# The experts' second layer in 320 and 192 columns instead of 256 and 256, with its weight units cut along k

## The chip, the cores and the metric

One core of one Trainium2 chip runs the whole program. The metric is the device time of one execution in microseconds (us); the times named here are of the kernel before. A profiled execution gives the trace, whose own clock starts at 0 and ends with the span.

## The reference, cut to what matters

Three layers follow each other: linear attention, a gated feed-forward layer, and a soft mixture of eight experts. Only the last one is touched:

```python
N, D, E, S_per_e, F = (2304, 512, 8, 4, 1024)
...
for e in range(E):
    h = np.maximum(slot_input[e] @ w1[e], 0.0)
    slot_out[e] = h @ w2[e]
slot_out = slot_out.reshape(n_slots, D)
c = logits - logits.max(1, keepdims=True)
c = np.exp(c)
c /= c.sum(1, keepdims=True) + 1e-09
return (c @ slot_out).astype(np.float32)
```

w1 and w2 are 16 MB each. An expert has four slots, so that its two products have four rows each; the combination `c @ slot_out` makes 2304 rows of 512 columns from 32 slots.

## The kernel before, in words

The front of the program (attention, the gated layer in six blocks of 384 tokens) is the same in both versions; the change lies in the tail, from about 680 us on, in the block that begins with `with ExitStack() as p3`.

**Weights.** w1 and w2 come in 32 units of 1 MB, a tile `eu` of 128 x 2048 each. `unit(n)` gives unit n and, where it isn't there yet, asks for all units up to n: each takes a place in one of the pools xw, wpA, wpB, xl (24 places in turn) and a load on SyncE's queue (L710). A load waits until the place's last reader is done. Units 0 to 15 are w1 (half of F, expert), 16 to 31 are w2. In w2, unit 16+e holds, for expert e, all eight k slices of 128 rows and the first 256 columns; unit 24+e holds the other 256 columns. Units 0 to 23 are asked for before the tail begins.

**First layer.** `fc1(e, half)` (L1081) multiplies the slots' inputs `xo` by one unit: four products of 512 columns, each in its own 32 output partitions. `turn1(half)` (L1086) copies the sums, turns them on TensorE (tile hp), adds over k and fills the tile `ho` with the ReLU. In the middle of the first half, before expert 4 (CTURN), `cturn` turns the last block's combine weights (ctp, cb), writes them to DRAM (`cT_d`, L826, on SyncE's queue) and `load_c` asks ScalarE's queue for both halves of the whole table cT, 432 KB each.

**Second layer.** `fc2(e, r, half)` (L1096) makes four of the eight k slices for expert e and column half r: four products of 256 columns into y2[r]. TensorE takes all of r = 0 first (eight experts with k slices 0 to 3, then eight with 4 to 7), then r = 1, expert by expert. A product of F32 operands stands in the trace as two records.

**Slots and combination.** `slots(r)` (L1103) copies y2[r] to SBUF, sums over partitions by a product with istack (tile so), and scales it into SO on VectorE in two operations. `combine(r, i)` (L1114) makes 256 tokens: two products of cT with SO (F32R, one record each), a copy from PSUM by VectorE or ScalarE in turn, and a transfer of 256 KB to `out` on SyncE's queue, in pieces of 1 KB. From expert 4 on (ELEFT), two combinations of r = 0 (NLEFT) follow each expert's products of r = 1; the last of them and all nine of r = 1 follow after `slots(1)`.

The order on an engine comes from a scheduler that goes by priorities; `placed(f, engine)` ties what f traces to the engine's last instruction, so that the written order stands there.

Of the kernel before, what the change touches and what calls it, by code (L numbers as in the profile page):

```python
# [7 lines left out]
F32 = mybir.dt.float32  # L8
# [3 lines left out]
ALU = mybir.AluOpType  # L12
# [15 lines left out]
LOW = 0.93 * 2.0 ** -29  # L28
KCONV, MCONV = (3, 2), (2, 2)
NX = 4  # L30
NLEFT = 2
ELEFT = 4
CTURN = 4
CEVERY = 3
PSLOTS = [1, 4, 7, 12, 14, 16, 18, 20, 24]
# [30 lines left out]
def tile_kernel(ctx: ExitStack, tc: tile.TileContext, q2T, qT, kT, v, wbd, wg, wv, wo, rmsg, phi, w1, w2, consts, out):  # L66
# [637 lines left out]
    def unit(n):  # L704
        while len(units) <= n:
            k = len(units)
            r, e = divmod(k, NE)
            u = upool[k % len(upool)].tile([128, 2048], F32, tag="w", name=f"eu{k}")
            src = (w1 if r < 2 else w2)[e, r % 2]
            SP.dma_start(out=u, in_=src)  # L710
            units.append(u)
        return units[n]
# [25 lines left out]
    with ExitStack() as p2:  # L738
# [10 lines left out]
        def post(blk, x2):  # L749
# [67 lines left out]
                DVE.tensor_copy(c3[:, :, 1], c3[:, :, 0])  # L817
                DVE.tensor_tensor(out=c3[:, :, 2].bitcast(F32R), in0=c, in1=c3[:, :, 0], op=ALU.subtract)

            def cturn(tp=None, keep=None):  # L820
                tp = tp or post_tile("ctp", [96, TPB, 128])
                for o in range(TPB):
                    PE.transpose(out=tp[:, o], in_=st["c3"][:, o].rearrange("p r s -> p (r s)"), identity=ident)
                cb = (keep or sp).tile([96, BLK], F32, tag="row", name="cb", bufs=1)
                DVE.tensor_copy(cb, tp.rearrange("p o t -> p (o t)"))
                SP.dma_start(out=cT_d[:, blk * BLK:(blk + 1) * BLK], in_=cb)  # L826

            def finish(acc, late):

# [235 lines left out]
    with ExitStack() as p3:  # L1065
        sp = pool(p3, "sp3")
        ps = pool(p3, "ps3", PSUM)
        y2 = [ps.tile([128, 256], F32, name=f"y2{r}") for r in range(2)]
        y1 = [ps.tile([128, 512], F32, tag="op", name=f"y1{r}", bufs=5) for r in range(2)]
        SO = sp.tile([96, 2, 256], F32R, name="SO")  # L1070
        cT = []

        ho = Own(8, wpA.tile([128, 8 * NE * NS], F32, tag="w", name="ho"))
# [1 line left out]
        def load_c():  # L1075
            for n in range(2):
                t = wpA.tile([128, NT // 2], F32R, tag="w", name="cT")[0:96]
                ACT.dma_start(out=t.bitcast(F32), in_=cT_d[:, NT // 2 * n:NT // 2 * n + NT // 2])
                cT.append(t)
# [14 lines left out]
            ho.fill(lambda o, i: ACT.activation(out=o, in_=i, func=AF.Relu), h, 4 * half, 4 * half + 4)  # L1094

        def fc2(e, r, half):  # L1096
            u = unit((2 + r) * NE + e).rearrange("p (k d) -> p k d", k=8)
            for c in range(4):
                k = 4 * half + c
                PE.matmul(out=y2[r][32 * c:32 * c + 32], lhsT=ho[e, k], rhs=u[:, k],  # L1100
                          start=e == 0 and half == 0, stop=e == NE - 1 and half == 1)

        def slots(r):  # L1103

            ysum = sp.tile([128, 256], F32, tag="y2s", name="y2s", bufs=1)
            DVE.tensor_copy(ysum, y2[r])
            so = ps.tile([96, 256], F32, tag="so", name="so", bufs=1)
            PE.matmul(out=so, lhsT=istack, rhs=ysum, start=True, stop=True)
            DVE.tensor_scalar(out=SO[:, r], in0=so, scalar1=rz, scalar2=None, op0=ALU.mult)
            DVE.scalar_tensor_tensor(out=SO[32:64, r], in0=so[32:64], scalar=rz[32:64], in1=SO[32:64, r].bitcast(F32), op0=ALU.mult, op1=ALU.subtract)  # L1110

        obs = {}

        def combine(r, i):  # L1114
            if i % 3 == 0:
                obs[r] = wpB.tile([128, 3, 2, 256], F32, tag="w", name="ob")
            ob = obs[r][:, i % 3]
            op = ps.tile([128, 2, 256], F32, tag="op", name="op", bufs=5)
            for n in range(2):
                t = 2 * i + n  # L1120
                PE.matmul(out=op[:, n], lhsT=cT[t // 9][:, 128 * (t % 9):128 * (t % 9) + 128], rhs=SO[:, r], start=True, stop=True)
            if i % 2:
                DVE.tensor_copy(ob, op)
            else:
                ACT.copy(out=ob, in_=op)
            SP.dma_start(out=out[256 * i:256 * i + 256, 256 * r:256 * r + 256].rearrange("(n p) d -> p n d", n=2), in_=ob)

        for e in range(NE):
            if e == CTURN:
                lastturn(ps.tile([96, TPB, 128], F32, tag="op", name="ctp", bufs=5), kl)  # L1130
                load_c()
            fc1(e, 0)
        fc1(0, 1)
        turn1(0)
        for e in range(1, NE):
            fc1(e, 1)
        for e in range(2):
            fc2(e, 0, 0)
        turn1(1)
        for e in range(2, NE):  # L1140
            fc2(e, 0, 0)
        for e in range(NE):
            fc2(e, 0, 1)
        first = [lambda i=i: combine(0, i) for i in range(TILES // 2)]
        for e in range(NE):
            fc2(e, 1, 0)
            fc2(e, 1, 1)
            if e == 0:
                slots(0)
            for f in first[:NLEFT] if e >= ELEFT else ():  # L1150
                f()
            first = first[NLEFT:] if e >= ELEFT else first
        slots(1)
        for f in first:
            f()
# [4 lines left out]
def _layout(inputs):  # L1160
    import numpy as np

    def heads(a):
# [22 lines left out]
        "rmsg": np.asarray(inputs["moe_rms_g"]).reshape(4, 128).T,  # L1186
        "phi": np.asarray(inputs["moe2_phi"]).reshape(4, 128, NS).transpose(1, 0, 2).reshape(128, 4 * NS),
        "w1": np.asarray(inputs["moe2_w1"]).reshape(NE, 4, 128, 2, 512).transpose(0, 3, 2, 1, 4).reshape(NE, 2, 128, 2048),
        "w2": np.asarray(inputs["moe2_w2"]).reshape(NE, 8, 128, 2, 256).transpose(0, 3, 2, 1, 4).reshape(NE, 2, 128, 2048),
        "consts": consts,  # L1190
    }

# [19 lines left out]
```

## Time and profile before

| what | value |
|---|---|
| time, median of 3 runs | 731.23 us (728.85 to 732.27) |
| the profiled execution's own time | 730.81 us |
| its span | 729.0 us, 11925 instructions |
| mean granted clock of TensorE | 0.991 |
| TensorE busy (PE) | 706.5 us, 97% |
| VectorE, ScalarE, GpSimd busy | 447.2, 340.5, 170.2 us |
| DMA of the whole span | 79.43 MB, mean 109 GB/s |
| chain that ended last, by engine | PE 84%, DVE 7%, ACT 4%, issue 2%, POOL 1%, DMA 1% |

The shares are averages over the whole program; TensorE is the bound of the six blocks, which the change leaves as they are. What counts here is the tail, where the weights of the experts come in and the result goes out; there the windows and the timelines of the single engines are read.

### The profile page before, as it was taken

Reading aid. Unit: us, or ns where it says so; the run is one execution under the profiler, and the core shown is the slowest. Engines: PE = TensorE matmul, PEld = TensorE weight load, DVE = VectorE, ACT = ScalarE, POOL = GpSimd, SP = SyncE. Lnnn points to the kernel's source line nnn. Section 1 sums busy time; section 2 is a strip of 40 time slices with the busy share of each in tenths; the row PEclk is TensorE's granted clock in tenths of the full one; section 3 lists DMA queues with packets and bytes.
Section 4 is the critical chain, followed back from the end, with each engine's and each line's share of the span. In section 5 each row is a group of like instructions: output and inputs, shape, how many; then the busy total and the mean of one; then the engine's idle time right before and its main releaser. Section 6 shows DMA issues by size and latency. Waiting matters only on the chain.

```text
span 729.0 us, 11925 instructions
## 1 busy us (share of the span) xinstructions
PE 706.5 (97%) x4713; PEld 575.7 (79%) x4713; DVE 447.2 (61%) x874; ACT 340.5 (47%) x711; POOL 170.2 (23%) x84
## 2 busy tenths in 40 slices
PE   6999999999999999999999999999999999999994
PEld 4657766988889888898889888899887999898343
DVE  5899755798655565566776666766667653233313
ACT  5896755698444554355531545415454131212103
POOL 0233200234101210124443244342443300000000
PEclk9999999999999999999999999999999999999898
DMA  8684214443011000100000100001000066576798
GB/s 315 215 293 171 88 37 160 150 181 119 1 62 39 27 22 23 39 22 22 23 1 9 44 22 23 1 9 33 23 1 1 9 259 260 201 261 265 280 371 273
DMA packets 25143, 79.43 MB, mean 109 GB/s; under 512 B 2688, under 2 KB 13376, under 8 KB 18688
## 3 DMA queue, kind: packets, MB, share of 16 engines
q1 hardware_dynamic: 24864, 77.79, 30.0%
q10 hardware_dynamic: 224, 0.88, 0.4%
q8 instruction: 37, 0.61, 0.3%
q14 instruction: 18, 0.15, 0.1%
HBM read 71.99 MB, written 6.67 MB: 108 GB/s over the span
## 4 chain that ended last, share of the span: by engine, by line
PE 84%; DVE 7%; ACT 4%; issue 2%; POOL 1%; DMA 1%; SPq 0%; DVEq 0%; POOLq 0%; ACTq 0%
PE pv L938 20%; PE pg L938 19%; PE acc L963 6%; PE acc L964 6%; PE acc L965 6%; PE num L221 4%; PE kacc L571 4%; PE y L1084 2%; PE P L526 2%; PE kacc L580 2%; PE y L1100 2%; DVE wt L154 2%; DVE wt L156 1%; PE o L472 1%; ACT wt L144 1%
## 5 line engine op out<-in xcount | busy, mean ns | idle before, releaser
L938 PE MATMUL pv<-xnh,wv 128*128 128x384 f32 x576 | 152.3, 345 | 0.0
L938 PE MATMUL pg<-xnh,wg 128*128 128x384 f32 x576 | 150.1, 342 | 0.5 <-DVE t L946 0.3
L938 PEld LDWEIGHTS pv<-xnh,wv 128*128 128x128 f32 x576 | 102.7, 188 | 12.3 <-issue 7.8
L938 PEld LDWEIGHTS pg<-xnh,wg 128*128 128x128 f32 x576 | 104.7, 188 | 6.2 <-ACT xnh L119 0.6
L938 PE MATMUL pv<-xnl,wv 128*128 128x384 f32 x288 | 97.8, 340 | 0.0
L938 PE MATMUL pg<-xnl,wg 128*128 128x384 f32 x288 | 97.5, 339 | 0.0
L963 PE MATMUL acc<-wo,hh 128*128 128x512 f32 x216 | 88.9, 412 | 0.0
L306 POOL PARTITION_ALL_REDUCE qe<-qe x32 | 51.3, 1603 | 155.1 <-ACT qe L305 155.1
L964 PE MATMUL acc<-wo,hh 128*128 128x512 f32 x216 | 85.8, 397 | 0.0
L965 PE MATMUL acc<-wo,hl 128*128 128x512 f32 x216 | 85.5, 396 | 0.0
L946 DVE SCALAR_TENSOR_TENSOR t<-t,pg 128x384 f32<-128x384 f32 x72 | 39.7, 551 | 70.1 <-ACT t L945 70.0
L119 ACT CAST hh<-t 128x384 fp32r<-128x384 f32 x72 | 36.8, 511 | 94.3 <-PE acc L964 73.6
L351 POOL PARTITION_ALL_REDUCE qe<-qe x24 | 61.9, 2626 | 71.3 <-DVE qe L350 41.8
L122 DVE TENSOR_TENSOR hl<-t,hh 128x384 fp32r<-128x384 f32 x72 | 41.8, 581 | 54.7 <-ACT hh L119 45.5
L945 ACT ACTIVATE t<-pg 128x384 f32<-128x384 f32 x72 | 35.2, 489 | 63.8 <-PE pg L938 63.7
L950 DVE TENSOR_TENSOR t<-t,pv 128x384 f32<-128x384 f32 x72 | 39.5, 549 | 30.3 <-PE pv L938 29.7
L938 PEld LDWEIGHTS pg<-xnl,wg 128*128 128x128 f32 x288 | 54.0, 188 | 0.5 <-DVE xnl L122 0.3
L938 PEld LDWEIGHTS pv<-xnl,wv 128*128 128x128 f32 x288 | 54.0, 188 | 0.4 <-issue 0.3
L965 PEld LDWEIGHTS acc<-wo,hl 128*128 128x128 f32 x216 | 40.5, 188 | 9.9 <-DVE hl L122 0.3
L963 PEld LDWEIGHTS acc<-wo,hh 128*128 128x128 f32 x216 | 40.7, 189 | 7.9 <-ACT hh L119 0.9
L964 PEld LDWEIGHTS acc<-wo,hh 128*128 128x128 f32 x216 | 40.7, 189 | 6.4
L571 PE MATMUL kacc<-kp,vt 128*64 128x256 f32 (+1 forms) x320 | 43.2, 393 | 1.9 <-ACT kp L548 1.4
(213 smaller groups left out, 1099.7 us busy)
## 6 DMA issues: line engine op xcount, KB each, us to landing
eu<-in_w_dram SPq DMA_DIRECT2D x32, 1024.0 KB, 6.5
wraw<-in_wg_dram SPq DMA_DIRECT2D x6, 1024.0 KB, 5.0
wraw<-in_wv_dram SPq DMA_DIRECT2D x6, 1024.0 KB, 5.4
wraw<-in_wo_dram SPq DMA_DIRECT2D x6, 1024.0 KB, 4.9
qraw<-in_qT_dram SPq DMA_DIRECT2D x32, 192.0 KB, 2.4
raw<-in_kT_dram SPq DMA_DIRECT2D x18, 256.0 KB, 3.9
vt<-in_v_dram SPq DMA_DIRECT2D x18, 256.0 KB, 3.5
out_dram<-ob SPq DMA_DIRECT2D x18, 256.0 KB, 3.2
```

The source lines that it names most:

```text
L119: ACT.copy(out=hi, in_=src)
L122: (lo_eng or POOL).tensor_tensor(out=lo, in0=src, in1=hi.bitcast(F32), op=ALU.subtract)
L306: POOL.partition_all_reduce(e[:, 0], e[:, 1], channels=128, reduce_op=bass_isa.ReduceOp.absmax)
L351: POOL.partition_all_reduce(e[hh][:, 1], u, channels=128, reduce_op=bass_isa.ReduceOp.add)
L571: PE.matmul(out=kva[o0:o0 + 64, hh // 2], lhsT=self.vt[r0:r1, h], rhs=kp[r0:r1, hh].rearrange("p s f -> p (s f)"), start=first and hh < 2, ...
L938: PE.matmul(out=p, lhsT=w[:, a, c], rhs=x, start=n == 0, stop=n == 11)
L945: ACT.activation(out=t, in_=g, func=AF.Tanh, scale=0.5)
L946: DVE.scalar_tensor_tensor(out=t, in0=t, scalar=1.0, in1=g, op0=ALU.add, op1=ALU.mult)
L950: DVE.tensor_tensor(out=t, in0=t, in1=wide("v", m, xs), op=ALU.mult)
L963: PE.matmul(out=acc[i], lhsT=hh[:, s], rhs=w[:, 0], start=m == 0, stop=False)
L964: PE.matmul(out=acc[i], lhsT=hh[:, s], rhs=w[:, 1], start=False, stop=False)
L965: PE.matmul(out=acc[i], lhsT=hl[:, s], rhs=w[:, 0], start=False, stop=m == MF - 1)
```

## The change

w2 is cut another way: unit 16+e holds the k slices 0 to 3 of expert e with all 512 columns, unit 24+e the k slices 4 to 7. The columns are parted in 320 (r = 0) and 192 (r = 1), so y2, SO and the sums get these widths. All 16 units are read by r = 0 and again by r = 1. Units 24 to 31 are asked for in the program right behind `fc1(e, 0)` (not behind expert 4) and `fc1(0, 1)`. The last block's `cT_d` write goes to ScalarE's queue, and `load_c` moves behind `fc1(2, 1)`. One combination of r = 0 follows each expert from expert 2 on. A combination of r = 0 has a PSUM tile and a copy of 320 columns for each 128 tokens, one of r = 1 a tile and a copy of 2 x 192. Pieces to `out` are 1280 and 768 bytes. Result tiles take places in wpA (first two) and wpB.

```diff
-NLEFT = 2
-ELEFT = 4
+RCOLS = [320, 192]
+ELEFT = 2
...
-            def cturn(tp=None, keep=None):
+            def cturn(tp=None, keep=None, queue=SP):
...
-                SP.dma_start(out=cT_d[:, blk * BLK:(blk + 1) * BLK], in_=cb)
+                queue.dma_start(out=cT_d[:, blk * BLK:(blk + 1) * BLK], in_=cb)
...
-        y2 = [ps.tile([128, 256], F32, name=f"y2{r}") for r in range(2)]
+        cols = [slice(sum(RCOLS[:r]), sum(RCOLS[:r + 1])) for r in range(2)]
+        y2 = [ps.tile([128, RCOLS[r]], F32, name=f"y2{r}") for r in range(2)]
...
-            u = unit((2 + r) * NE + e).rearrange("p (k d) -> p k d", k=8)
+            u = unit((2 + half) * NE + e).rearrange("p (k d) -> p k d", k=4)
             for c in range(4):
-                k = 4 * half + c
-                PE.matmul(out=y2[r][32 * c:32 * c + 32], lhsT=ho[e, k], rhs=u[:, k],
+                PE.matmul(out=y2[r][32 * c:32 * c + 32], lhsT=ho[e, 4 * half + c], rhs=u[:, c, cols[r]],
                           start=e == 0 and half == 0, stop=e == NE - 1 and half == 1)
...
+            ob = rows(i)[:, :, cols[r]]
+            per = 512 // RCOLS[r]
+            for n in range(0, 2, per):
+                op = ps.tile([128, per, RCOLS[r]], F32, tag="op", name="op", bufs=5)
+                for m in range(per):
+                    t = 2 * i + n + m
+                    PE.matmul(out=op[:, m], lhsT=cT[t // 9][:, 128 * (t % 9):128 * (t % 9) + 128], rhs=SO[r], start=True, stop=True)
+                if (i + n) % 2:
+                    DVE.tensor_copy(ob[:, n:n + per], op)
+                else:
+                    ACT.copy(out=ob[:, n:n + per], in_=op)
+            SP.dma_start(out=out[256 * i:256 * i + 256, cols[r]].rearrange("(n p) d -> p n d", n=2), in_=ob)
...
             if e == CTURN:
-                lastturn(ps.tile([96, TPB, 128], F32, tag="op", name="ctp", bufs=5), kl)
-                load_c()
+                lastturn(ps.tile([96, TPB, 128], F32, tag="op", name="ctp", bufs=5), kl, ACT)
             fc1(e, 0)
+            if e < NX or e > NX:
+                unit(len(units))
         fc1(0, 1)
+        unit(len(units))
         turn1(0)
         for e in range(1, NE):
             fc1(e, 1)
+            if e == 2:
+                load_c()
...
         for e in range(NE):
-            fc2(e, 0, 1)
+            placed(lambda: fc2(e, 0, 1), PE.engine)
         first = [lambda i=i: combine(0, i) for i in range(TILES // 2)]
         for e in range(NE):
-            fc2(e, 1, 0)
-            fc2(e, 1, 1)
+            placed(lambda: fc2(e, 1, 0), PE.engine)
+            placed(lambda: fc2(e, 1, 1), PE.engine)
             if e == 0:
-                slots(0)
-            for f in first[:NLEFT] if e >= ELEFT else ():
-                f()
-            first = first[NLEFT:] if e >= ELEFT else first
+                placed(lambda: slots(0), PE.engine)
+            if e >= ELEFT:
+                placed(first.pop(0), PE.engine)
```

The change moves work in three orders. On SyncE's queue the loads of units 24 to 31 (eu24 to eu31, the number behind the name is the tile's) stood around the write of the last combine weights. Before:

```order
L710 DMA eu23_6482<-in_w2_dram 128x2048
L710 DMA eu24_6747<-in_w2_dram 128x2048
L826 DMA cT_d_79<-cb_6606 96x384
L710 DMA eu25_6763<-in_w2_dram 128x2048
L710 DMA eu26_6773<-in_w2_dram 128x2048
```

The same stretch with the change:

```order
L710 DMA eu23_6482<-in_w2_dram 128x2048
L710 DMA eu24_6591<-in_w2_dram 128x2048
L710 DMA eu25_6597<-in_w2_dram 128x2048
L710 DMA eu26_6603<-in_w2_dram 128x2048
L710 DMA eu27_6609<-in_w2_dram 128x2048
```

The write is gone from this queue, and the eight loads follow each other. On ScalarE the loads of cT stood before and behind the copy of the first layer's sums (ys). Before:

```order
L1078 DMA cT_6609<-cT_d_79 96x1152
L1088 COPY ys_6633<-y10_6581 128x512
L1078 DMA cT_6611<-cT_d_79 96x1152
L1094 ACTIVATE ho_6584<-h_6640 128x7x4x4
L1094 ACTIVATE ho_6584<-h_6640 128x4x4
L1094 ACTIVATE ho_6584<-h_6687 128x7x4x4
L1094 ACTIVATE ho_6584<-h_6687 128x4x4
```

The same stretch with the change:

```order
L826 DMA cT_d_79<-cb_6615 96x384
L1089 COPY ys_6646<-y10_6581 128x512
L1095 ACTIVATE ho_6585<-h_6653 128x7x4x4
L1095 ACTIVATE ho_6585<-h_6653 128x4x4
L1095 ACTIVATE ho_6585<-h_6704 128x7x4x4
L1095 ACTIVATE ho_6585<-h_6704 128x4x4
L1079 DMA cT_6665<-cT_d_79 96x1152
L1079 DMA cT_6667<-cT_d_79 96x1152
```

The write stands there now ahead of ys, and both loads of cT stand behind the second filling of ho. On TensorE the second layer's end (y20 is y2[0], y21 is y2[1]) and the first combinations (op) before:

```order
L1100 MATMUL y20_6579<-eu23_6482,ho_6584 32x256 x4
L1100 MATMUL y21_6580<-eu24_6747,ho_6584 32x256 x8
L1108 MATMUL so_6759<-y2s_6757,cst_72 96x256
L1100 MATMUL y21_6580<-eu25_6763,ho_6584 32x256 x8
L1100 MATMUL y21_6580<-eu26_6773,ho_6584 32x256 x8
L1100 MATMUL y21_6580<-eu27_6783,ho_6584 32x256 x8
L1100 MATMUL y21_6580<-eu28_6793,ho_6584 32x256 x8
L1121 MATMUL op_6804<-SO_6583,cT_6609 128x256 x2
L1121 MATMUL op_6809<-SO_6583,cT_6609 128x256 x2
L1100 MATMUL y21_6580<-eu29_6814,ho_6584 32x256 x8
```

The same stretch with the change:

```order
L1100 MATMUL y20_6579<-eu31_6644,ho_6585 32x320 x4
L1100 MATMUL y21_6580<-eu16_6384,ho_6585 32x192 x4
L1100 MATMUL y21_6580<-eu24_6591,ho_6585 32x192 x4
L1109 MATMUL so_6774<-y2s_6772,cst_72 96x320
L1100 MATMUL y21_6580<-eu17_6386,ho_6585 32x192 x4
L1100 MATMUL y21_6580<-eu25_6597,ho_6585 32x192 x4
L1100 MATMUL y21_6580<-eu18_6388,ho_6585 32x192 x4
L1100 MATMUL y21_6580<-eu26_6603,ho_6585 32x192 x4
L1128 MATMUL op_6795<-SO0_6583,cT_6665 128x320
L1128 MATMUL op_6798<-SO0_6583,cT_6665 128x320
L1100 MATMUL y21_6580<-eu19_6430,ho_6585 32x192 x4
```

Unit 31 is now the last that r = 0 reads, ahead of every product of r = 1; the first combination stands behind three experts instead of five, and single combinations and experts take turns.

## Rows read from the trace of the kernel before

**Rows 1.** Windows: us, busy us by engine (instructions), PE clock, DMA share, GB/s

```profile
690.00:700.00 10.00, 10.00 (x104) 3.62 (x100) 1.95 (x3) 0.99 (x3) 0.00 (x0) 1.00 1.02 345
...
705.00:710.00 5.00, 5.00 (x86) 2.71 (x82) 1.38 (x3) 0.00 (x0) 0.00 (x0) 1.00 1.01 418
711.70:719.30 7.60, 6.37 (x69) 4.20 (x62) 4.14 (x8) 2.93 (x7) 0.00 (x0) 1.00 0.76 253
719.30:725.70 6.40, 1.54 (x11) 1.19 (x10) 2.13 (x4) 2.11 (x5) 0.00 (x0) 0.76 1.02 340
```

**Rows 2.** Timeline of TensorE in the tail (start us, us, line, operation, tiles, shapes, count)

```profile
686.70 4.50 PE L1084 MATMUL y<-eu,xo 128*32 128x512 f32 x40
691.13 0.66 PE L1091 MATMUL hp<-cst,ys 128*128 128x128 f32 x4
...
697.75 1.05 PE L1100 MATMUL y<-eu,ho 128*32 128x256 f32 x16
...
699.33 7.11 PE L1100 MATMUL y<-eu,ho 128*32 128x256 f32 x128
706.37 0.67 PE L1108 MATMUL so<-y2s,cst 128*96 128x256 f32 x2
706.98 3.66 PE L1100 MATMUL y<-eu,ho 128*32 128x256 f32 x64
710.57 0.74 PE L1121 MATMUL op<-SO,cT 96*128 96x256 f32 x4
711.24 1.07 PE L1100 MATMUL y<-eu,ho 128*32 128x256 f32 x16
712.24 0.74 PE L1121 MATMUL op<-SO,cT 96*128 96x256 f32 x4
...
718.21 2.63 PE L1121 MATMUL op<-SO,cT 96*128 96x256 f32 x18 [1.23 <-DVE SO L1110]
```

**Rows 3.** Timeline of VectorE in the tail

```profile
705.65 0.42 DVE L1106 COPY y2s<-y 128x256 f32<-128x256 f32 x1 [5.52 <-PE y L1100]
707.09 0.48 DVE L1109 TENSOR_SCALAR SO<-so,small 96x256 fp32r<-96x256 f32 x1 [1.01 <-PE so L1108]
707.60 0.48 DVE L1110 SCALAR_TENSOR_TENSOR SO<-so,small,SO 32x256 fp32r<-32x256 f32 x1
```

**Rows 4.** Timeline of ScalarE, the second filling of ho

```profile
700.16 0.40 ACT L1094 ACTIVATE ho<-h 128x112 f32<-128x112 f32 x2 [7.16 <-DVE h L1093]
```

**Rows 5.** Timeline of SyncE in the tail; a row spans several issues

```profile
682.37 0.33 SPq L710 DMA_DIRECT2D eu<-in_w_dram  x1
687.39 0.33 SPq L826 DMA_DIRECT2D cT_d<-cb  x1
687.81 10.57 SPq L710 DMA_DIRECT2D eu<-in_w_dram  x7
711.73 13.93 SPq L1126 DMA_DIRECT2D out_dram<-ob  x18
```

**Rows 6.** Tile eu, the load issued at 682.4 and its landing

```profile
L710 SPq DMA_DIRECT2D eu<-in_w_dram x1: 328/328/328, 682.4 to 682.4; - x1
...
DMA to landing us min/median/max: 4.9/4.9/4.9
```

**Rows 7.** Tile eu, the last load, issued at 698.0, and its landing

```profile
L710 SPq DMA_DIRECT2D eu<-in_w_dram x1: 327/327/327, 698.0 to 698.0; - x1
...
DMA to landing us min/median/max: 15.7/15.7/15.7
```

**Rows 8.** Tile cT, its two loads and their landing

```profile
L1078 ACTq DMA_DIRECT2D cT<-cT_d x2: 311/349/387, 688.7 to 690.6; - x2
...
DMA to landing us min/median/max: 9.3/10.6/12.0
```

**Rows 9.** Tensor out, the last two transfers and their landing

```profile
L1126 SPq DMA_DIRECT2D out_dram<-ob x2: 685/688/691, 724.2 to 725.0; - x2
...
DMA to landing us min/median/max: 3.2/3.2/3.3
```

More of the change, by code (lines that the diff above doesn't have):

```diff
@@ L1067, in tile_kernel @@
         ps = pool(p3, "ps3", PSUM)
-        y2 = [ps.tile([128, 256], F32, name=f"y2{r}") for r in range(2)]
+        cols = [slice(sum(RCOLS[:r]), sum(RCOLS[:r + 1])) for r in range(2)]
+        y2 = [ps.tile([128, RCOLS[r]], F32, name=f"y2{r}") for r in range(2)]
         y1 = [ps.tile([128, 512], F32, tag="op", name=f"y1{r}", bufs=5) for r in range(2)]
-        SO = sp.tile([96, 2, 256], F32R, name="SO")
+        SO = [sp.tile([96, RCOLS[r]], F32R, name=f"SO{r}") for r in range(2)]
         cT = []
@@ L1103, in slots @@
         def slots(r):
-            ysum = sp.tile([128, 256], F32, tag="y2s", name="y2s", bufs=1)
+            w = RCOLS[r]
+            ysum = sp.tile([128, RCOLS[0]], F32, tag="y2s", name="y2s", bufs=1)[:, 0:w]
             DVE.tensor_copy(ysum, y2[r])
-            so = ps.tile([96, 256], F32, tag="so", name="so", bufs=1)
+            so = ps.tile([96, RCOLS[0]], F32, tag="so", name="so", bufs=1)[:, 0:w]
             PE.matmul(out=so, lhsT=istack, rhs=ysum, start=True, stop=True)
-            DVE.tensor_scalar(out=SO[:, r], in0=so, scalar1=rz, scalar2=None, op0=ALU.mult)
@@ L1110, in slots, with rows @@
-            DVE.scalar_tensor_tensor(out=SO[32:64, r], in0=so[32:64], scalar=rz[32:64], in1=SO[32:64, r].bitcast(F32), op0=ALU.mult, op1=ALU.subtract)
+            DVE.tensor_scalar(out=SO[r], in0=so, scalar1=rz, scalar2=None, op0=ALU.mult)
+            DVE.scalar_tensor_tensor(out=SO[r][32:64], in0=so[32:64], scalar=rz[32:64], in1=SO[r][32:64].bitcast(F32), op0=ALU.mult, op1=ALU.subtract)
         obs = {}
-        def combine(r, i):
[L1115 to L1126, printed above, removed]
+        def rows(i):
+            j = i // 2
+            if j not in obs:
+                obs[j] = (wpA if j < 2 else wpB).tile([128, 2, 2, DM], F32, tag="w", name="ob")
+            return obs[j][:, i % 2]
@@ L1188, in _layout @@
         "w1": np.asarray(inputs["moe2_w1"]).reshape(NE, 4, 128, 2, 512).transpose(0, 3, 2, 1, 4).reshape(NE, 2, 128, 2048),
-        "w2": np.asarray(inputs["moe2_w2"]).reshape(NE, 8, 128, 2, 256).transpose(0, 3, 2, 1, 4).reshape(NE, 2, 128, 2048),
+        "w2": np.asarray(inputs["moe2_w2"]).reshape(NE, 2, 4, 128, 512).transpose(0, 1, 3, 2, 4).reshape(NE, 2, 128, 2048),
         "consts": consts,
```

## The prediction

> **What bounds the kernel now.** Only the tail is touched, so I read its timelines first and its windows second. TensorE's timeline [rows 2] shows it working from 686.7 us on with no idle time in brackets until the last group of combinations at 718.21, which waits 1.23 us for SO. So up to there TensorE's own work sets the pace, and no weight unit is late. A product has two records, and records go by columns: 40 of 512 columns take 691.13 - 686.70 = 4.43 us, 111 ns each; 128 of 256 columns take 706.37 - 699.33 = 7.04 us, 55.0 ns each [rows 2]. Behind TensorE stands the writing of the result. The 18 issues begin at 711.73 [rows 5], the last stands at 725.0 and lands 3.2 us later, at 728.2 [rows 9]; the span ends 0.8 us after that. From 719.3 on the DMA engines are full (share 1.02) at 340 GB/s [rows 1]: a transfer of 262,144 bytes takes 0.77 us there, and 18 of them 13.8 us. The whole writing lasts 728.2 - 711.73 = 16.5 us, so 2.7 us of it are idle time and latency. The window 711.7 to 719.3 tells where: share 0.76, so 0.24 x 7.6 = 1.8 us without work [rows 1]. The end is thus set by when the first transfer starts, by 13.8 us of transfers, and by gaps in between.
>
> **The change part by part.** The sum is made against the profiled execution's 730.81 us, 0.4 us under the median of 731.23.
>
> *First half of the columns.* The 64 products (128 records) of r = 0 grow from 256 to 320 columns: 128 x (68.8 - 55.0) ns = 1.8 us more on the path. Those of r = 0 end now at about 699.33 + 112 x 0.055 = 705.5, with the change at 707.3. No row has 320 columns; 55.0 and 111 ns bound it, and as these two stand in the ratio 1 to 2, I take the line between them.
>
> *Second half.* 128 records of 192 columns take 41.3 ns by the same line, 0.66 us for an expert's 16 instead of 0.88, 1.8 us less in all. The bounds: 41.3 ns, and 55.0 if something other than columns is the floor there.
>
> *To the first combination.* y2s follows the products of r = 0 by 0.15 us and takes 0.42 us [rows 3]; with 320 columns I take 0.49, so it is done at 707.9. By then TensorE has made expert 0 of r = 1 (0.66 us). The sum over partitions took 706.37 to 707.05, 0.68 us [rows 2]; with 320 columns 0.85, so 708.8. SO takes two operations of 0.48 us and small gaps, 707.09 to 708.08 [rows 3]; with 320 columns 0.55 each, so 710.0. TensorE makes experts 1 and 2 meanwhile, 0.1 + 2 x 0.66 us, and comes to the first combination at 710.2: neither waits for the other. Its two products and the copy of 320 columns (0.49) take 0.9 us, where before two products and a copy of 512 took 711.73 - 710.57 = 1.16 [rows 2, 5]. First issue at 711.1, 0.6 us earlier than before.
>
> *The pace of the first six.* Now each expert's 16 records are followed by one combination. An expert alone between combinations takes 712.24 - 711.24 = 1.00 us where 16 x 55.0 ns are 0.88, and two combinations take 711.24 - 710.57 = 0.67 us where the last group needs 2.63 / 18 = 0.146 us a product, 0.58 for four [rows 2]. So each change between the two kinds costs about 0.1 us. That gives 0.66 + 0.12 for an expert and half of 0.67 plus 0.05 for a combination: 1.16 us a pair. A transfer of 327,680 bytes takes 0.92 us. I get this from two rows: 1 KB pieces at 340 GB/s are 48 ns a piece and engine, 8 KB pieces at 418 GB/s [rows 1] are 314 ns; the line between gives 57.5 ns for 1280 bytes and 38.5 for 768, times 16 pieces an engine. Idle: 5 x (1.16 - 0.92) = 1.2 us. The sum of all transfers stays: 9 x (0.92 + 0.62) = 13.8 us. Against the 1.8 us of before, less some 0.7 for starting up and with 0.3 for the last unit's remains, 1.4, the gaps shrink by 0.2 us. The sixth is issued at 711.1 + 5 x 1.16 = 716.9.
>
> The Trainium skill, page TensorEngine Tiling (Array Packing), section Key Properties, says that changing the tiling mode drains TensorE. It speaks against this change, which goes from 32-wide to 128-wide products and back twice more often in the loop. The trace agrees: those 0.1 us a change [rows 2]. Without that drain the pair would take 0.96 us, the transfers would leave almost no gap, and the sum would be 1.0 us better.
>
> *Behind the loop.* r = 1 ends near 716, then four products of r = 0, the second sum, four more, and the second SO, with copies of r = 0 between on VectorE; I put the first combination of 192 columns at 718.9, where that of 256 stood at 718.21 [rows 2]. That costs nothing: nine transfers of r = 0 keep the DMA engines busy until 711.1 + 9 x 0.92 + 1.2 = 720.6, and the first result of r = 1 is there near 719.8. If that cover were gone, each us later would show. Combinations of 192 columns: 0.146 us a product at best (the row of 256), and at worst what the F32 sum took for its one product of 256 columns, 0.68 us, so 0.51 for 192; nine transfers of 0.62 hide the first, not the second.
>
> *The loads.* Unit 24 was asked for at 682.37 and landed 4.9 us later, 687.3 [rows 5, 6]. Behind it the cT_d write held SyncE's queue until 687.39; seven more followed until 698.0 [rows 5], and the last landed at 713.7 [rows 7], just ahead of its product. With the change the write is on ScalarE's queue, before the copy of ys, which has to wait for its sums anyway. Units 25 to 31 wait for products of fc1 that end one after the other up to the hp at 691.13 [rows 2], so all are asked for by about 691.5. At 418 GB/s a unit takes 2.51 us: 687.3 + 7 x 2.51 = 704.8. Needed is unit 31 with the last expert of r = 0, at 707.3 - 8 x 0.069 = 706.7. So the loads fit, by 1.9 us.
>
> *cT.* Both loads now stand behind the second filling of ho, at 700.6 [rows 4], 10 to 12 us later than before. They took 9.3 and 12.0 us to land among the units [rows 8]; the first combination wants the first at 710.2. Alone behind unit 31 (0.88 MB, 2.1 us) both are there by 708. With 12.0 us it would be 712.6, 2.4 us late: the bound. I take 0, since but one or two units are still on their way.
>
> Sum: first transfer -0.6, gaps -0.2, transfers 0, loads and cT 0: **-0.8 us**, 730.0 for the profiled execution, **730.4 us** on the median's scale. Best case: no gap at all, -0.6 - 1.4 = -2.0, 729.2.
>
> **The rivals.** *The last units come late (slower).* The price is TensorE standing before the last expert of r = 0. Before, seven units and cT took 713.7 - 687.8 = 25.9 us [rows 5, 7], and in 690 to 700 the rate was 345 GB/s [rows 1], not 418. If cT is served wholly before unit 31, it costs its 2.1 us and some 1.8 us of that lower rate: 708.7, 2.0 us late, 731.2 + 1.2 = 732.4. If seven units and cT take as long as before, from 687 on, unit 31 lands at 712.9, 6.2 us late: 736.6. It decides from 706.7 on, and costs more than it brings from 707.5. For it: the loads run back to back with cT beside them. Against: cT is asked for when the units are nearly through. The Trainium skill, page DMA: Bandwidth & Descriptors, section Queues, rings and completion order, says that an engine takes turns between its queues; the 9.3 to 12.0 us of cT agree [rows 8]. By that rule alone cT, asked for at 700.7, goes half and half with the last units, and the time is that 732.4.
>
> *Narrow products cost as much as those of 256.* Then r = 1 loses its 1.8 us, a pair takes 1.38 us, the gaps grow by 1.1 and the first transfer comes 0.4 later: 731.9; with combinations of 192 at 0.51 us a product, nine of them take 9.2 us against 5.6 of transfers, and the last result comes about 2.9 us after that of the forecast: 733.3. For it: no row is narrower than 256 on all four column groups. Against: exact proportion between 256 and 512.
>
> *The writing is not what ends it.* If the idle time of before is latency that stays, only 0.6 us or nothing is won: 730.6 to 731.2.
>
> **How the numbers follow.** About 0.5%, 3.7 us, is what a measurement of this kernel can tell from no change. Chances: the forecast with its best case 0.60 (729.2 to 731.2), nothing won 0.10, cT ahead of unit 31 0.12 (732.4), narrow products 0.10 (732 to 733.3), units as slow as before 0.05 (736.6), something larger on the good side that no row shows 0.03. Three runs of before lie within 728.85 to 732.27, so a median may stand 1.5 us off. The range goes from 727.8 (729.2 less the scatter) to 733.5 and leaves out the last two cases and some scatter. Faster by over 0.5% needs 727.5, beyond the best case: 0.07 with the scatter. Slower needs 734.9: 0.08. The rest is 0.85.
>
> **What would show it.** Right: records of 320 and 192 columns start 69 and 41 ns apart; no idle time before products of r = 0; the first issue to `out` near 711, and full DMA engines from 717 to the end. Wrong: idle time before a product that reads unit 31 or cT; 1.4 us a pair; a gap of the DMA engines between r = 0 and r = 1. A time under 727.5 would mean that something before 711 got shorter, which I don't see.

## The result and the profile after

| | time, median of 6 runs | lowest to highest |
|---|---|---|
| before | 730.37 us | 727.90 to 732.27 |
| after | 735.62 us | 734.10 to 737.48 |

The ratio after to before is 1.0074, 95% interval [1.0050, 1.0099]: slower by some 5.3 us, 0.7%, where 730.4 had been forecast with a range up to 733.5. The profiled execution took 735.43 us, its span is 733.6 us, the mean granted clock 0.987.

TensorE's timeline of the tail answers to [rows 2] (start us, us, what; in brackets the idle time ahead and what ended it):

```profile
697.78 7.21 PE L1100 MATMUL y<-eu,ho 128*32 128x320 f32 x104
708.87 2.58 PE L1100 MATMUL y<-eu,ho 128*32 128x320 f32 x24 [3.89 <-DMA eu<-in_w_dram]
...
712.69 2.07 PE L1100 MATMUL y<-eu,ho 128*32 128x192 f32 x32
714.69 0.56 PE L1128 MATMUL op<-SO,cT 96*128 96x320 f32 x2
...
723.87 2.25 PE L1128 MATMUL op<-SO,cT 96*128 96x192 f32 x18 [1.00 <-DVE SO L1111]
```

Two things are there that the kernel before doesn't have. Ahead of the last expert's products of r = 0 TensorE stands 3.89 us for a load. And the 24 records behind it, eight of 320 and sixteen of 192 columns, take 2.58 us, where the rows ahead give 7.21 / 104 = 69 ns for one of 320 columns and so some 1.3 us for all. The windows (us, busy us by engine, clock, DMA share, GB/s; they answer to [rows 1]) say why:

```profile
705.00:710.00 5.00, 1.13 (x12) 0.55 (x16) 0.00 (x0) 0.00 (x0) 0.00 (x0) 0.71 0.40 106
710.00:715.00 5.00, 5.00 (x56) 2.43 (x48) 1.58 (x3) 0.00 (x0) 0.00 (x0) 0.61 0.00 0
715.00:720.00 5.00, 5.00 (x73) 2.78 (x72) 1.97 (x4) 1.70 (x4) 0.00 (x0) 1.00 0.52 183
720.00:725.00 5.00, 4.00 (x38) 3.19 (x38) 3.88 (x9) 2.59 (x7) 0.00 (x0) 1.00 0.84 288
725.00:730.00 5.00, 1.11 (x10) 0.94 (x9) 1.52 (x4) 1.62 (x4) 0.00 (x0) 0.75 1.02 329
```

In 705 to 710 the granted clock is 0.71 in the mean, in 710 to 715 it is 0.61, after that 1.00 until the last products are done. TensorE worked without idle time up to 704.99. Windows of 1 us show that the clock fell while it stood, and when it rose again:

```profile
706.00:707.00 1.00, 0.00 (x0) 0.00 (x0) 0.00 (x0) 0.00 (x0) 0.00 (x0) 1.00 0.75 195
707.00:708.00 1.00, 0.00 (x0) 0.00 (x0) 0.00 (x0) 0.00 (x0) 0.00 (x0) 0.53 0.15 58
...
713.00:714.00 1.00, 1.00 (x20) 0.64 (x16) 0.89 (x2) 0.00 (x0) 0.00 (x0) 0.56 0.00 0
```

At about 707.07, 2.1 us into the wait, it went to 0.50, the lower of its two levels, 1.2 of 2.4 GHz; at about 713.9, after 5.0 us of work at that level, it was back at 1.00. And the DMA engines move nothing at all from 710 to 715: everything is in, and nothing can go out yet.

SyncE's queue [rows 5] and the loads of the units [rows 6, 7]:

```profile
680.75 9.09 SPq L710 DMA_DIRECT2D eu<-in_w_dram  x8
715.84 14.65 SPq L1133 DMA_DIRECT2D out_dram<-ob  x18
```

```profile
L710 SPq DMA_DIRECT2D eu<-in_w_dram x8: 327/328/328, 680.8 to 689.5; - x8
...
DMA to landing us min/median/max: 4.7/10.4/19.2
```

All eight units are asked for by 689.6, the first one lands 4.7 us after its issue, at 685.5, near the 4.9 us of the forecast. The last one lands 19.2 us after its issue, at 708.7. The chain of waits names it:

```profile
689.51 19.22 DMA eu<-in_w_dram
708.74 0.14 issue
```

The front of the program, which the change leaves alone, differs by some 4 us from one profiled execution to the next: the second layer's first product starts between 694.77 and 698.64 in the 13 traces of this study. The profile is of one execution, too, and not always of a typical one: that of experiment 1 is the fastest of its 12 (730.25, median 732.15), that of experiment 5 nearly the slowest (732.33, median 730.90). So I compare lengths from that product on, and take the times from the medians. Before, it starts at 697.75 and the span ends at 729.0: 31.25 us. After, 696.00 to 733.6: 37.6 us, 6.35 more. The wait is 3.9 of that. The low clock is 2.3: from unit 31's product to the first combination it is 714.69 - 708.87 = 5.82 us here and 3.50 in the first experiment at full clock.

### The profile page after: what moved, and what is told of

Its sections match the earlier page's. It is cut to its first block, busy times and chain, and to the rows that moved or that the text cites. A ratio compares the mean times of both kernels' runs of the same rounds, so it can differ in the third digit from the quotient of the medians.

```text
span 733.6 us, 11935 instructions
## 1 busy us (share of the span) xinstructions
PE 708.0 (97%) x4713; PEld 575.8 (78%) x4713; DVE 448.0 (61%) x879; ACT 340.7 (46%) x715; POOL 170.0 (23%) x84
## 4 chain that ended last, share of the span: by engine, by line
PE 83%; DVE 6%; ACT 4%; DMA 3%; issue 2%; POOL 1%; SPq 0%; DVEq 0%; POOLq 0%; ACTq 0%
PE pv L938 20%; PE pg L938 19%; PE acc L963 6%; PE acc L964 6%; PE acc L965 6%; PE num L221 4%; PE kacc L571 4%; DMA eu<-in_w_dram 3%; PE P L526 2%; PE kacc L580 2%; PE y L1085 1%; PE y L1100 1%; DVE wt L156 1%; PE o L472 1%; DVE wt L154 1%
## 5 line engine op out<-in xcount | busy, mean ns | idle before, releaser
L938 PEld LDWEIGHTS pv<-xnh,wv 128*128 128x128 f32 x576 | 102.6, 188 | 12.3 <-issue 7.8
```

Of the source, the lines that this page charges most:

```text
L938: PE.matmul(out=p, lhsT=w[:, a, c], rhs=x, start=n == 0, stop=n == 11)
```

## The experiments

In all of them the ratio is to the kernel before, run on the same chip beside it. The first four went together. Theory A: unit 31 is late since cT moves beside it, and TensorE's standing costs the clock as well. Theory B: the unit is late by itself, since the DMA engines don't finish together. Theory C: the columns cost something, apart from any load.

**1. cT behind unit 31 on the same queue.** If cT's packets between those of unit 31 make it late, they are to queue up behind it.

```diff
-                ACT.dma_start(out=t.bitcast(F32), in_=cT_d[...])
+                SP.dma_start(out=t.bitcast(F32), in_=cT_d[...])
```

> Both loads of cT go on SyncE's queue, right behind the load of unit 31, instead of on ScalarE's queue. Theory A (cT, taken in turn with the last units, makes unit 31 late): unit 31 is through 4 us after unit 30's pace would say at most, near 704 in this trace's time, TensorE waits 0 to 0.5 us before it, the clock stays at 2.4 GHz, and the time falls by the 3.9 us of the wait and the 2.2 us of low clock behind it: 735.6 - 6 = 729.5 us. Rival B (one of the DMA engines is behind anyway, for instance by fetches of code, and cT only fills what is idle): unit 31 still comes at 707 to 708, the wait stays over 2.5 us, 734 to 736 us. Rival C (the narrow second half costs it, and the wait is hidden elsewhere): wait gone, but time above 733.

Measured: 732.15 us, ratio 1.0042 [1.0025, 1.0060]. TensorE's timeline:

```profile
706.03 1.40 PE L1100 MATMUL y<-eu,ho 128*32 128x320 f32 x24 [2.22 <-DMA eu<-in_w_dram]
...
709.53 0.56 PE L1128 MATMUL op<-SO,cT 96*128 96x320 f32 x2
```

The wait is 2.22 us instead of 3.89, the clock is 1.00 in every window from 700 to 720, and so the same 24 records take 1.40 us. That cT made the unit later is thereby shown; that this isn't all, too. Neither expectation was met: 729.5 us was asked of theory A, a wait of over 2.5 of theory B.

**2. TensorE kept at work.** 20 products of 512 columns that nobody reads, ahead of unit 31's.

```diff
+            if e == NE - 1:
+                placed(busy, PE.engine)
             placed(lambda: fc2(e, 0, 1), PE.engine)
```

> The changed kernel with 20 products of 512 columns more (results unused) ahead of the products of unit 31, 40 records x 0.111 = 4.4 us, about as long as TensorE waits there. Theory A with the clock: unit 31 is as late as before (708 to 709), but the granted clock stays at 1.00 from 705 to 715, the products behind it run at 69 and 41 ns a record, and the 2.2 us are won back, less 0.5 that the added work is longer than the wait: 733.9 us. If the low clock costs nothing on the path (for instance because the transfers to out set the end): 735.6 to 736.1 us.

Measured: 733.92 us, ratio 1.0063 [1.0041, 1.0085]. Timeline and windows:

```profile
703.96 4.47 PE L1140 MATMUL busy<-eu,ho 128*32 128x512 f32 x40
708.45 1.40 PE L1100 MATMUL y<-eu,ho 128*32 128x320 f32 x24
...
711.95 0.56 PE L1128 MATMUL op<-SO,cT 96*128 96x320 f32 x2
```

```profile
705.00:710.00 5.00, 4.99 (x58) 1.80 (x50) 0.49 (x1) 0.00 (x0) 0.00 (x0) 1.00 0.27 80
710.00:715.00 5.00, 5.00 (x74) 2.72 (x74) 2.07 (x4) 0.91 (x3) 0.00 (x0) 1.00 0.20 68
```

Unit 31's product starts as late as in the change, at 708.45 against 708.87, but TensorE didn't stand, the clock stays at 1.00, and the first combination comes 3.50 us later and not 5.82. The low clock is shown to be a cost of its own, 2.3 us by the traces, and standing to be what brings it. The time shows less of it (the ratios differ by 0.0011, 0.8 us, and their intervals overlap), partly because the filler itself lasted too long: its products end 13.7 us behind the second layer's first, and the change's wait ended at 12.9.

**3 and 4. Equal columns.** The change with 256 and 256 columns: units, early loads and order stay. Once as the change has cT, once with cT as in experiment 1.

```diff
-RCOLS = [320, 192]
+RCOLS = [256, 256]
```

> The changed kernel with 256 and 256 columns; cut of the weights, loads and order stay. Theory A: unit 31 comes at the same time, but r = 0 is through 1.6 us earlier, so TensorE waits some 5.5 us and has 1.8 us more to do behind it: about 1.5 us slower than the change, 737 us. Rival C (the split in 320 and 192 costs the time by itself): faster than the change, 730 to 733 us.

> 256 and 256 columns and cT on SyncE's queue. Theory A: unit 31 lands near 704.5, needed near 703.4: a wait of about 1 us and little or no low clock; then r = 1 takes 1.8 us more than with 192 columns, but starts earlier: 729.5 to 731.5 us, level with or above the run with 320 and 192 columns. Rival C: clearly under that run.

Measured: 738.24 us, ratio 1.0113 [1.0089, 1.0136], and 734.82 us, 1.0075 [1.0053, 1.0097]. By the ratios both are slower than their twins with 320 and 192 columns, by 0.0039 and 0.0033, 2.8 and 2.4 us. The intervals just overlap, but the lengths from the second layer's first product say the same: 40.3 us against 37.6, and 34.9 against 33.7. For the second run 729.5 to 731.5 had been expected, with a wait of about 1 us; the wait was 2.85. TensorE and windows of the first, then TensorE of the second:

```profile
705.20 0.64 PE L1100 MATMUL y<-eu,ho 128*32 128x256 f32 x8 [2.12 <-DMA eu<-in_w_dram]
709.89 2.79 PE L1100 MATMUL y<-eu,ho 128*32 128x256 f32 x24 [4.06 <-DMA eu<-in_w_dram]
```

```profile
705.00:710.00 5.00, 0.75 (x12) 0.29 (x16) 0.00 (x0) 0.00 (x0) 0.00 (x0) 0.72 0.45 134
710.00:715.00 5.00, 5.00 (x50) 2.14 (x53) 1.38 (x3) 0.00 (x0) 0.00 (x0) 0.60 0.00 0
```

```profile
708.77 1.50 PE L1100 MATMUL y<-eu,ho 128*32 128x256 f32 x24 [2.85 <-DMA eu<-in_w_dram]
...
712.67 0.50 PE L1128 MATMUL op<-SO,cT 96*128 96x256 f32 x2
```

So theory C falls: with unit 31 late, the uneven columns are no part of the loss, they bring something (whether they would with no load late was not run). Since a load sets when r = 0 ends, columns moved into r = 0 are made inside the wait, and less is left behind it. From the first combination to the end it is 20.7 us here in both (712.67 to 733.4 in the second) against 18.9 with 320 and 192.

**5. cT held until unit 31 is in.** Experiment 1 left 2.2 us of wait, and cT's packets may still reach DMA engines that are done with unit 31 while others aren't. Here ScalarE copies a column of unit 31 first.

```diff
         def load_c():
+            g = sp.tile([128, 1], F32, tag="gate", name="gate", bufs=1)
+            ACT.copy(out=g, in_=unit(4 * NE - 1)[:, 0:1])
             for n in range(2):
...
-                load_c()
+                placed(load_c, ACT.engine)
```

> The change, with ScalarE made to copy one column of unit 31 before it issues the two cT loads, so that no byte of cT moves until the unit is in. Theory A (the cT packets between its own are what is left of unit 31's lateness behind SyncE's run of the first experiments): unit 31 lands 2.5 to 2.7 us behind unit 30, the wait before its product is about 1.2 us, the clock stays at 1.00, and the time is 731 (first combination 0.5 to 1 us later than it could be, since cT now lands last). Theory B (the last unit is late by itself, since one of the 16 DMA engines lags behind the others, whatever else is in the queues): unit 31 still lands 3.3 us or more behind unit 30, the wait stays at 2.0 us or more, and the time is 732 to 732.5.

Measured: 730.90 us, ratio 1.0008 [0.9993, 1.0023]. TensorE, and windows around unit 31's landing:

```profile
707.25 1.40 PE L1102 MATMUL y<-eu,ho 128*32 128x320 f32 x24 [0.63 <-DMA eu<-in_w_dram]
...
711.69 0.53 PE L1130 MATMUL op<-SO,cT 96*128 96x320 f32 x2 [0.88 <-DMA cT<-cT_d]
```

```profile
700.00:704.00 4.00, 4.00 (x64) 1.93 (x60) 0.21 (x1) 0.40 (x2) 0.00 (x0) 1.00 1.01 428
704.00:705.00 1.00, 1.00 (x20) 0.52 (x16) 0.00 (x0) 0.00 (x0) 0.00 (x0) 1.00 0.79 320
705.00:706.00 1.00, 1.00 (x21) 0.49 (x16) 0.00 (x0) 0.00 (x0) 0.00 (x0) 1.00 0.18 74
706.00:707.00 1.00, 0.62 (x12) 0.03 (x4) 0.00 (x0) 0.00 (x0) 0.00 (x0) 1.00 0.04 16
```

By the time theory A stands (though the profiled execution is 1.4 us above the median), by the mechanism it falls half: the wait is 0.63 us, but the unit landed at 707.1 (issued at 691.1, 16.0 us), still 2.5 us behind a landing at full rate (682.2 + 4.8 + 17.6 = 704.6). The windows show how: up to 704 the engines are full at 428 GB/s, and then they have not finished together. In the last two microseconds 0.18 and 0.04 of them work, three of sixteen and then less than one, with no byte of cT about. So theory B's lagging engines exist.

The packets of the trace show what holds the last one. In them a unit's load ends with 16 packets of 4 bytes, one for each engine, so that the spread of these ends can be followed from unit to unit. For unit 27 they lie between 694.61 and 696.04; for unit 28 fifteen lie between 697.06 and 698.50 and one at 699.23, and it stays that far behind up to unit 31: fifteen have ended by 705.86, the last at 706.67. In between, one packet of instruction loading (queue q8) starts at 697.15 and takes 0.98 us, and the packet of the unit right behind it takes 0.80 us instead of 0.31: 1.47 us that one engine lost. The DMA view of 697 to 699 has that one packet, 3.0% of 16 engines' 2 us:

```profile
q8 instruction: 1, 0.02, 3.0%
```

Which engine a packet ran on is inferred from starts that follow ends. In ten traces, those of the change and of experiments 1 to 9, such a packet starts between 693.5 and 697.6 and the one behind it takes 0.77 to 0.81 us. So the engine with the instructions ends 0.8 us behind the others here, more than the whole wait of 0.63; no run is without that packet, so this is read from the trace and not tried.

Some 1.2 of the 2.5 us are in all engines: between the mean ends of units 24 and 31 lie 18.8 us and not 17.6, most of it in unit 25 (3.35 us where the later ones take 2.5) and in unit 26, among whose packets the last cT_d write goes (112 packets, 0.40 us of each engine). And cT, now last, makes the first combination wait 0.88 us.

**6 and 7. Products of r = 1 ahead of unit 31's.** All units' first k halves are in by then, so the eight experts' r = 1 products of that half can fill the wait; once with cT as in the change, once with cT held.

```diff
+            if e == NE - 1:
+                for k in range(NE):
+                    placed(lambda: fc2(k, 1, 0), PE.engine)
             placed(lambda: fc2(e, 0, 1), PE.engine)
...
-            placed(lambda: fc2(e, 1, 0), PE.engine)
```

> The change, with all eight experts' r=1 products of the first k half (32 products of 192 columns at 41.3 ns a record, 2.65 us) put ahead of unit 31's first product; the loop then keeps only the second k half. Theory A (unit 31 is late and TensorE idles for it, and the idle time then costs the clock): unit 31 lands as late as in the change, the wait falls from 3.9 to about 1.1 us, the granted clock stays at 1.00 from 705 to 715, the loop's combinations come closer together by 0.33 us a turn, and the time is 731 to 732. Rival (the time is lost behind the loop, in the writing, and the wait is hidden in it anyway): the wait falls as said, but the time stays at 734 or more.

> Both of the two edits before: the cT loads held until unit 31 is in, and the r=1 products of the first k half ahead of unit 31's. Theory A: the wait before unit 31's product is gone (1.2 less 2.65), the clock stays, the combinations start when cT is in; from the second layer's first product to the end 30.5 us against 31.25 in the kernel before, so 729 to 729.5: the change is worth its 0.8 us of writing once its loads are not waited for. Rival (the 320 and 192 columns or the earlier loads cost something by themselves): 731 or more.

Measured: 732.67 us, ratio 1.0024 [1.0009, 1.0039], and 731.44 us, 1.0010 [0.9996, 1.0023]. The waits for the unit are gone in both, and the clock stays at 1.00. But 729 was not reached, nor 731 to 732 in the first. TensorE of the second:

```profile
700.41 10.67 PE L1102 MATMUL y<-eu,ho 128*32 128x320 f32 x184
711.37 0.78 PE L1111 MATMUL so<-y2s,cst 128*96 128x320 f32 x2 [0.29 <-DVE y2s L1109]
...
713.41 0.53 PE L1130 MATMUL op<-SO,cT 96*128 96x320 f32 x2 [0.48 <-DVE SO L1113]
```

The first combination stands 713.41 - 698.64 = 14.8 us behind the second layer's first product, later than in experiment 5 (14.1). Filling 0.6 us of waiting with 2.65 us of products puts r = 0's end off by 2 us. I had counted the wait that goes and not the end that moves.

**8. The early loads alone.** The kernel before with its own columns and units, but with its last eight units and cT asked for as in the change.

```diff
-            def cturn(tp=None, keep=None):
+            def cturn(tp=None, keep=None, queue=SP):
...
+            if e < NX or e > NX:
+                unit(len(units))
...
+            if e == 2:
+                load_c()
```

> The kernel before, with its columns and weight units as they are, but its last eight units asked for as early as in the change (one behind each of the first layer's products), the last cT write on ScalarE's queue and the cT loads asked for behind the first layer's third expert. All of r=0 then needs only units 16 to 23, which are in long before. Theory A (only the need for all sixteen units before r=0 can end makes the loads late): no wait before the r=0 products, no fall of the clock, 730 and within 0.5% of the kernel before. Rival (asking early by itself crowds the queues or delays the cT loads): 732 or more.

Measured: 729.68 us, ratio 0.9999 [0.9982, 1.0016]; 31.2 us from the second layer's first product to the end, as before. Its last unit lands as late as the change's (issued at 689.6, 19.4 us), and nobody waits for it, for its columns are wanted only with r = 1. The early loads cost nothing; needing them all before r = 0 can end does.

**9. Four experts ahead of unit 31 instead of eight,** the other products of r = 1 beside the SO chain and one in each turn of the loop; cT held. The edit is shown against experiment 7.

```diff
-                for k in range(NE):
+                for k in range(4):
                     placed(lambda: fc2(k, 1, 0), PE.engine)
...
-            placed(lambda: fc2(e, 1, 1), PE.engine)
+            if e < 2:
+                placed(lambda: fc2(4 + 2 * e, 1, 0), PE.engine)
+                placed(lambda: fc2(5 + 2 * e, 1, 0), PE.engine)
+            if e == 1:
+                placed(lambda: fc2(0, 1, 1), PE.engine)
+            if e > 0:
+                placed(lambda: fc2(e, 1, 1), PE.engine)
...
-            if e >= ELEFT:
+            if e >= ELEFT - 1:
```

> The change with the cT loads held until unit 31 is in, four experts' r=1 products of the first k half ahead of unit 31's (1.32 us, in place of eight and 2.65 us), the other four and two experts' second halves beside the chain that makes SO, and one second half in each turn of the loop. Theory (in the run with eight ahead, the wait was gone but r=0 ended as much later as products were put ahead of it): no wait before unit 31's product, the first combination 14.0 us behind the second layer's first product (when cT is in) in place of 14.8, the pace 0.95 us, from that first product to the end 31.4 us in place of 32.2, and 0.8 us less than the run with eight: 730.6, the same as the kernel before. Rival (r=0's end is not what sets the writing's start): 731.5 as with eight.

Measured: 730.02 us, ratio 1.0002 [0.9984, 1.0020].

```profile
700.41 9.70 PE L1102 MATMUL y<-eu,ho 128*32 128x320 f32 x160
...
712.21 0.56 PE L1130 MATMUL op<-SO,cT 96*128 96x320 f32 x2
...
713.16 0.56 PE L1130 MATMUL op<-SO,cT 96*128 96x320 f32 x2
...
720.83 2.24 PE L1130 MATMUL op<-SO,cT 96*128 96x192 f32 x18 [1.45 <-DVE SO L1113]
```

No wait, the first combination at 712.21 - 698.63 = 13.6 us, the turn at 0.95 us, 31.5 us to the end: as expected, and no better than the kernel before. What the loop saves, the last group gives back in part: it waits 1.45 us for the second SO where the change waits 1.00.

**10. Without unit 31.** This prices the change with no load late; the kernel leaves unit 31 out, and expert 7's products read unit 30 in its place.

```diff
+            if k == 4 * NE - 1:
+                units.append(units[k - 1])
+                break
```

> The change without its last weight unit: unit 31 is not loaded, and the products of expert 7's second k half read unit 30 (so that half of the expert is left out, and another one's is used in its place). Everything else is the change's, the cT loads included. What this prices is the change when no load is late. Theory A (only the late unit, and the clock behind it, cost): no wait before the last r=0 products, the clock at 1.00, and from the second layer's first product to the end 31.5 us (the run with held cT loads took 33.0, with 0.6 and 0.9 us of waits in it), against 31.25 in the kernel before: 729.5 to 730.5, so that the forecast gain of 0.8 us is not there even then, because the loop's pace is 1.28 and not 1.16 us a combination. Rival (the forecast's sum was right but for the loads): 30.5 us and 729.5 or less. Other rival (the columns or units cost something else): 731.5 or more.

Measured: 730.93 us, ratio 1.0012 [0.9998, 1.0027].

```profile
699.56 8.39 PE L1103 MATMUL y<-eu,ho 128*32 128x320 f32 x128
...
708.63 1.51 PE L1103 MATMUL y<-eu,ho 128*32 128x192 f32 x32
710.07 0.56 PE L1131 MATMUL op<-SO,cT 96*128 96x320 f32 x2
710.56 0.86 PE L1103 MATMUL y<-eu,ho 128*32 128x192 f32 x16
711.35 0.56 PE L1131 MATMUL op<-SO,cT 96*128 96x320 f32 x2
```

No idle time, full clock, and 697.79 to 729.0 is 31.2 us, the 31.25 of before. So the forecast's gain would not have come even with the loads in time: 0.8 us less would be a ratio of 0.9989, below the interval.

**11. Experiment 9's order without unit 31,** cT early as in the change (its diff is those of 9 and 10, without the held cT); like 10 it leaves unit 31 out.

> The order of products of the run before, without unit 31 (as in the run that leaves it out, the products of expert 7's second k half read unit 30) and with the cT loads asked for as early as in the change: no load is late, and the loop's pace is set by the writing. It prices what is the most that this arrangement could give. Expected: first combination 13.5 us behind the second layer's first product, 17.4 us from it to the end, 30.9 in all against 31.25 in the kernel before: 0.3 us, 729.5 to 730, which can't be told from no change. Rival (the loads' lateness is not the limit): no less than the run with four ahead and all units.

Measured: 731.24 us, ratio 1.0015 [0.9997, 1.0032]; 696.15 to 727.9 is 31.75 us, not the 30.9 expected. The first combination came at 13.8 us, not 13.5, and the 17.4 us of writing in experiment 7 don't carry over: here, as in 9, the second SO comes 1.45 us late, 18.0. No version beat the kernel before.

## Why the prediction was wrong

| from the second layer's first product, us | to the first combination | from there to the end | sum | wait for unit 31 | ratio |
|---|---|---|---|---|---|
| before | 12.8 | 18.4 | 31.2 | none | 1 |
| after | 18.7 | 18.9 | 37.6 | 3.9 and low clock | 1.0074 |
| 1, cT on SyncE | 14.7 | 19.0 | 33.7 | 2.2 | 1.0042 |
| 5, cT held | 14.1 | 18.9 | 33.0 | 0.6 | 1.0008 |
| 9, four filled | 13.6 | 17.9 | 31.5 | none | 1.0002 |
| 10, no unit 31 | 12.3 | 18.9 | 31.2 | none | 1.0012 |

The lengths are of one profiled execution each, the ratios of the medians.

**The step that failed is "So the loads fit, by 1.9 us".** From the first landing plus 7 x 2.51 us it would be 685.4 + 17.6 = 703.0 in this execution, and TensorE came to unit 31's product at 704.99: the same room, 2.0 us. Unit 31 landed at 708.7, 5.7 us later. From 690 to 703, while units alone moved, the rate itself was right. Windows of the change:

```profile
690.00:700.00 10.00, 10.00 (x113) 3.73 (x116) 2.08 (x3) 0.81 (x4) 0.00 (x0) 1.00 1.01 423
700.00:703.00 3.00, 3.00 (x52) 1.47 (x48) 0.00 (x0) 0.00 (x0) 0.00 (x0) 1.00 1.04 411
703.00:706.00 3.00, 1.99 (x32) 0.70 (x24) 0.00 (x0) 0.00 (x0) 0.00 (x0) 1.00 1.02 271
706.00:709.00 3.00, 0.13 (x4) 0.16 (x8) 0.00 (x0) 0.00 (x0) 0.00 (x0) 0.68 0.32 90
```

411 to 423 GB/s up to 703. Then cT joins, and the engines are as full (1.02) but move 271 GB/s: a third less. The DMA view of 702 to 709 (packets, MB, share of 16 engines) has cT in q10:

```profile
q10 hardware_dynamic: 224, 0.88, 46.6%
```

46.6% of 7 us are 3.3 us of all engines: a cT packet of 4608 bytes takes 0.27 us in the mean, one of a unit's, of 8192 bytes, mostly 0.31. I had let cT cost the 2.1 us of its bytes at 418 GB/s, and nothing for unit 31, "since but one or two units are still on their way"; but those two are the ones that count. The same sum, first issue + first landing + 17.6 us, says for each run how late its last unit was: 5.7 here, 5.5, 6.5, 3.9 and 6.1 in experiments 2, 3, 6 and 8 with cT beside it (mean 5.5), 3.3, 3.6, 2.5, 3.0 and 2.0 in 1, 4, 5, 7 and 9 with cT behind it (mean 2.9). So cT is about half, and the other half is there without it. Experiment 5 parts that half again: some 1.2 us that all engines need longer than 7 x 2.51 us, the cT_d write among them, which the sum had moved to another queue at no price, and some 1.2 us by which the last engine falls back further, most of it for one packet of instructions. In the change the two meet: fifteen engines are through with unit 31 by 706.17, and the one with the instruction packet, which was 1.05 us behind them at unit 28, at 708.28. A forecast by the mean rate can't see that; a load is in when the last engine is through. The rows of before showed only that the last unit took 15.7 us from issue to landing [rows 7], and I had put that down to its place in the queue.

**No case had the clock.** The rival "the last units come late" had the mechanism. But it had 2.0 us of standing and a chance of 0.12; the wait was 3.9, and it brought 2.3 more by the low clock. Its second price, seven units and cT as slow as before (6.2 us late, 736.6, chance 0.05), comes nearest to the time of 735.6, but by luck: it had 6.2 us of wait, where 3.9 were wait and 2.3 the clock. Waits of 2.2 and 2.85 us (experiments 1 and 4) brought no fall; 3.9 us (the change) and 4.06 (experiment 3, which had one of 2.12 just ahead) did. The length of a wait alone doesn't tell: in the change the clock fell 2.1 us into it, in experiment 3 1.3 us into the second, and in experiment 4 it stayed up through 2.85. What decides that is open here. The Trainium skill, page DMA: Bandwidth & Descriptors, section Queues, rings and completion order, says that an engine takes turns between its queues; unit 31's greater lateness wherever cT is asked for beside it agrees, and I had given that rule too little weight.

**The sum of -0.8 had one term mis-sized, the pace.** The first transfer's -0.6 held: in experiment 10 the first issue to out comes 711.22 - 697.79 = 13.43 us after the first product, before 711.73 - 697.75 = 13.98. The gaps were to shrink by 0.2 and grew: from first combination to end 18.9 against 18.4 us. A pair takes 1.28 us (710.07 to 711.35), not 1.16. The expert's 16 records take 0.79 us with the change of tiling, as forecast; the combination takes 0.49 where I had put half of 0.67 plus 0.05, 0.385, and so charged a product of 320 columns what one of 256 costs. By columns it is 0.42 + 0.05. Five gaps of 0.12 more are 0.6 of the 0.7 us. (The 0.7 for starting up and the 0.3 for the last unit's remains, which the sum took off the 1.8 of before, stood on no row.) With -0.55 and +0.5 the change is worth nothing, and 6.35 = 3.9 + 2.3 + 0.15 for what is left over.

**Right were:** records by columns (69 and 41 ns: 104 of 320 columns in 7.21 us; in experiment 7, 112 of 320 and 72 of 192 in 10.67), so the rival of narrow products is out, as it is for the combinations, whose last 18 take 2.25 us and not 9.2; in experiment 4 a pair with 256 columns takes 1.43 us; the first combination, 12.28 us behind the second layer's first product in experiment 10 and 12.82 before; and that TensorE would not wait for cT where it is asked for early. The cover "behind the loop" held: the last group waits 1.00 us where it waited 1.23 [rows 2], with the DMA engines at 1.02 from 725 to 730.

## What to carry to other kernels

Changing how weights are cut changes when each piece is needed: units cut along the sum are all needed before the first result, units cut along the columns only half of them, and the other half arrives while results already go out. Put the landing of the last piece against its first use with the slowest DMA engine and every other transfer of that moment in the sum, not the mean rate. And a filler ahead of a late product is worth only as much as the wait; beyond it, it moves the end that everything behind waits for.

## What the runs showed of the hardware

- Standing costs twice. In waits of 3.9 and 4.06 us (the change and experiment 3) the granted clock fell to 0.50, 2.1 and 1.3 us into the wait, and stayed there for 5.0 and 4.1 us of the work behind it; in the change 3.5 us of work took 5.8. In waits of 2.2 and 2.85 us it stayed at 1.00, and so it did where 4.5 us of products that nobody reads stood in the gap.
- DMA engines that share one load don't finish together: in experiment 5 the last 2 us of unit 31 ran with 0.18 and 0.04 of them busy. The loads' mean rate of 428 GB/s held until 704, and the unit landed at 707.1. One packet of instruction loading of 0.98 us, with a slow packet of 0.80 behind it, cost its engine 1.47 us, and that engine ended 0.8 us behind the other fifteen.
- Full engines say nothing of bytes: a share of 1.01 was 423 GB/s with units alone, one of 1.02 was 271 GB/s with cT among them, whose packets of 4608 bytes took 0.27 us where 8192 bytes took 0.31.
